# A hand-made start for an attention and feed-forward kernel: loads in order of need, the first group's attention by hand, integer work on GpSimd

## The chip, the core and the metric

The kernel runs on one core of a Trainium2 chip. The metric is the device time of one execution in microseconds. A core has five engines that run side by side, each through its own instructions in order: TensorE (PE in the profile; weight loads are shown as PEld), VectorE (DVE), ScalarE (ACT), GpSimd (POOL) and SyncE (SP), which here only issues transfers. They meet through semaphores. TensorE writes its results to PSUM[...].

## The reference

Attention without a softmax, for 8 groups (the batch) of 8 heads, 576 rows and 64 columns a head, then a feed-forward layer on 4608 tokens:

```python
kv  = einsum('bhsd,bhse->bhde', k, v)          # 64 x 64 a head
out = einsum('bhsd,bhde->bhse', q, kv)
rms = sqrt(mean(out * out, axis=-1) + 1e-6)
x   = (out / rms * g_norm)                     # -> (4608, 512)
h   = x @ w_in                                 # 512 -> 2048
g   = h * erf(softplus(h))
y   = g @ w_out                                # 2048 -> 512, (4608, 512) float32
```

q, k and v are float32. w_in and w_out are float64[...]: each weight comes in as two 32-bit integers, and the kernel makes a float32 of them.

## The kernel before

Two heads are a pair; a group of the batch has four pairs (`NP`), each giving 128 of the 512 columns of `xT`. For every pair there are four pieces of work, shortened here:

```python
def products():                                   # piece 0
    kv_ps = bank("kv_ps")
    for c in range(C):                            # C = 6 in the first group, two heads: 12 products
        ... nc.tensor.matmul(kv_ps[s, s], lhsT=ks[rows, i, c], rhs=vs[rows, i, c], ...)
    if p % 2 == 0:                                # the last 64 rows of q, for two pairs at once
        nc.tensor.transpose(kv_ps[:, q_tail], q_last[:, p // 2], ident)
    ...
    nc.vector.tensor_copy(out=bd[s, s], in_=kv_ps[s, s])          # two copies
    if p % 2 == 0:
        nc.vector.tensor_copy(out=tails[T], in_=kv_ps[:, q_tail])
    qt_ps = bank("qt_ps")
    for j in range(J):                            # J = 4
        nc.tensor.transpose(qt_ps[:, j * P : j * P + P], qs[:, j], ident)
    nc.scalar.copy(st["qT"], qt_ps)

def apply():                                      # piece 1
    nc.tensor.matmul(kv_ps[:, o_tail], lhsT=bd, rhs=st.pop("tail"), start=True, stop=True)
    nc.tensor.matmul(o_ps, lhsT=bd, rhs=qT, start=True, stop=True)     # o_ps is bank("se_ps")
    nc.vector.tensor_copy(out=x_last[:, p, T * R : T * R + R], in_=kv_ps[:, o_tail])
    nc.scalar.activation(qT, o_ps, AF.Square)

def mean():                                       # piece 3
    nc.tensor.matmul(ms, lhsT=mean_w.bitcast(FP32), rhs=u, start=True, stop=True)
    nc.scalar.activation(r, ms, AF.Ln, bias=eps_col)
    nc.scalar.activation(r, r, AF.Exp, scale=-0.5)
    nc.scalar.activation(u, r, AF.Square)

def norm():                                       # piece 4: three VectorE operations, the last writes xT
    ...(out=u, in0=ms, scalar=EPS, in1=u, op0=ALU.add, op1=ALU.mult)
    ...(out=u, in0=u, scalar=3.0, in1=r, op0=ALU.subtract, op1=ALU.mult)
    ...(out=x, in0=o, scalar=gm_col, in1=u, op0=ALU.mult, op1=ALU.mult)
```

A weight tile goes through load, split and join. The first four tiles (w0 to w3 here) are of w_in and hold 128 x 512 weights; later ones hold 128 x 1024.

```python
def w_split(which, f, k):
    nc.vector.tensor_scalar(out=e, in0=hi, scalar1=20, scalar2=0x7FF, op0=logical_shift_right, op1=bitwise_and)
    nc.scalar.activation(e, e, AF.Relu, scale=float(1 << 23), bias=exp_col)
    nc.vector.tensor_scalar(out=m, in0=hi, scalar1=0xFFFFF, scalar2=None, op0=bitwise_and)
    nc.scalar.activation(m.bitcast(FP32), m, AF.Identity, scale=2.0**-20, bias=1.0)

def w_join(which, f, k):                          # three VectorE operations
    ...(out=e, in0=hi, scalar=-(1 << 31), in1=e, op0=bitwise_and, op1=bitwise_or)
    ...(out=m, in0=lo, scalar=2.0**-52, in1=m, op0=mult, op1=add)
    nc.vector.tensor_tensor(out=out_, in0=e, in1=m, op=mult)      # out_: w_in_sb or w_out_sb
```

The start, in the order in which it is given to the engines:

```python
for i in range(NP - 1):                           # q on SP; k, v of pairs 0 to 2 on ACT's queue
    load_pair(i)
    if i == 0:
        load_last(0, 0); load_last(0, 1)
...
for _ in range(2):
    w_next("load")
load_last(0, 2); load_last(0, 3)
load_pair(NP - 1)
w_rounds = {1: ("split",), 2: ("join", "load", "split"), 3: ("join", "load"),
            5: ("split",), 6: ("split", "join", "load", "join", "load")}
banks_0 = {"kv_ps": (ps_at, "at"), "qt_ps": (ps_h, "h"), "ms_ps": (ps_h, "h")}
first = [attention(0, p, banks_0 | {"se_ps": (ps_o, f"o{p}")}) for p in range(NP)]
for i in range(NP + 3):
    for piece, p in ((0, i), (1, i - 1), (4, i - 3), (3, i - 2)):
        if 0 <= p < NP:
            first[p][piece]()
    ...
    for what in w_rounds.get(i, ()):
        w_next(what)
```

Behind it stands a loop over the hidden columns (`h_ps`, line 692): columns 0 and 1 need xT of all four pairs and weight tiles w0 and w1, column 2 needs w2, column 3 w3. Meanwhile the next group's attention and more splits and joins go on. The rest of the kernel, from the third group on, is the same products in three-part fp32r form (line 462).

## Time and profile before

| | |
|---|---|
| time, median of 3 runs | 944.4 us (943.82 to 945.24) |
| span of the profiled execution | 942.4 us |
| TensorE busy | 924.8 us, 98% |
| VectorE busy | 742.6 us, 79% |
| ScalarE busy | 615.6 us, 65% |
| GpSimd busy | 2.4 us, 10 instructions |
| first product of a pair starts | 6.49 us |
| first hidden column starts | 27.54 us (weight load), third 35.95 us |
| HBM over the span | 275 GB/s |

A row of the timeline reads: start in us, duration, engine, line of the kernel, operation, out<-in by the program's names, shape, number of instructions, and in brackets how long the engine was idle before and what released it. A row of a table of windows reads: the stretch, its length, busy time and number of instructions of PE, PEld, DVE, ACT and POOL, the granted clock, the share of the 16 DMA engines, GB/s. A row of the waits names who waited for whom, the sum, the number and the longest. "q" behind an engine's name is its sequencer.

### The profile page before, as it was taken

The page shows a single profiled execution, that of the slowest core. Times are in us where ns is not written, and L with a number is a line of the kernel's source. Part 1 is how long each engine was busy: PE and PEld are TensorE (multiplying, and loading weights), DVE is VectorE, ACT ScalarE, POOL GpSimd, SP SyncE. Part 2 cuts the span into 40 slices and gives each one's busy share as a digit, 9 for nine tenths or more (in the row PEclk, how much of TensorE's full clock was granted, in tenths as well). Part 3 has the DMA queues.
Part 4 walks back from the last instruction along what each step waited for, and adds up shares of the span by engine and source line. Part 5 has one row for each costly group of instructions (what it writes and reads, how often), then busy time and mean ns, then how long its engine had stood idle before and what let it go on. Part 6 is the DMA issues. An engine that isn't in the chain of part 4 may idle for free.

```text
span 942.4 us, 11743 instructions
## 1 busy us (share of the span) xinstructions
PE 924.8 (98%) x4272; PEld 683.4 (73%) x4272; DVE 742.6 (79%) x1056; ACT 615.6 (65%) x825; POOL 2.4 (0%) x10
## 2 busy tenths in 40 slices
PE   6999999999999999999999999999999999999997
PEld 4444445666688888888888888888888888888886
DVE  3999858887577787877778888878887877787667
ACT  3899776776766666666666666666666666665551
POOL 1000000000000000000000000000000000000000
PEclk9999999999999999999999999999999999999999
DMA  9766406899699998998899889998896778778871
GB/s 257 276 204 207 150 1 227 318 351 335 214 363 335 309 325 283 306 311 307 280 287 314 294 298 309 311 303 296 293 325 260 263 253 345 284 286 287 353 263 46
DMA packets 111842, 259.78 MB, mean 276 GB/s; under 512 B 43864, under 2 KB 69544, under 8 KB 111784
## 3 DMA queue, kind: packets, MB, share of 16 engines
q1 hardware_dynamic: 110152, 256.73, 78.7%
q10 hardware_dynamic: 1568, 2.29, 0.8%
q8 instruction: 34, 0.56, 0.2%
q14 instruction: 24, 0.20, 0.1%
q0 software_dynamic: 64, 0.00, 0.0%
HBM read 224.40 MB, written 34.60 MB: 275 GB/s over the span
## 4 chain that ended last, share of the span: by engine, by line
PE 92%; DVE 4%; DMA 2%; ACT 1%; issue 0%; SPq 0%; DVEq 0%
PE n_ps L462 45%; PE m_ps L462 22%; PE o_ps L520 10%; PE h_ps L692 6%; PE se_ps L325 3%; PE kv_ps L297 2%; PE qt_ps L319 2%; DMA w_raw<-in_moe_w_in_dram 1%; PE ms_ps L351 1%; DMA v_sb<-in_v_dram 1%; DVE h L876 1%; DVE e L445 1%; PE ms_ps L346 1%; PE ms_ps L347 1%; PE kv_ps L324 1%; DVE e L440 0%
## 5 line engine op out<-in xcount | busy, mean ns | idle before, releaser
L462 PE MATMUL n_ps<-x_forms,w_in_parts 128*128 128x512 f32 x896 | 232.5, 401 | 0.1
L462 PE MATMUL n_ps<-w_out_parts,g_forms 128*128 128x512 f32 x928 | 231.2, 391 | 0.0
L462 PEld LDWEIGHTS n_ps<-w_out_parts,g_forms 128*128 128x128 f32 x928 | 174.2, 188 | 38.4 <-issue 1.4
L462 PEld LDWEIGHTS n_ps<-x_forms,w_in_parts 128*128 128x128 f32 x896 | 166.8, 188 | 43.1 <-issue 9.3
L852 ACT ACTIVATE s<-h 128x512 f32<-128x512 f32 x112 | 71.0, 633 | 178.9 <-DVE h L445 178.9
L445 DVE TENSOR_TENSOR h<-m_ps,h 128x512 f32<-128x512 f32 x116 | 79.7, 687 | 59.8 <-ACT h L837 43.8
L462 PE MATMUL m_ps<-w_out_parts,g_forms 128*128 128x512 f32 x464 | 124.2, 389 | 0.0
L462 PE MATMUL m_ps<-x_forms,w_in_parts 128*128 128x512 f32 x448 | 120.0, 390 | 0.0
L520 PE MATMUL o_ps<-w_out_sb,h_sb 128*128 128x512 f32 x224 | 100.8, 593 | 0.3 <-DVE h_sb L642 0.3
L462 PEld LDWEIGHTS m_ps<-w_out_parts,g_forms 128*128 128x128 f32 x464 | 87.1, 188 | 18.0
L462 PEld LDWEIGHTS m_ps<-x_forms,w_in_parts 128*128 128x128 f32 x448 | 84.1, 188 | 17.7
L445 DVE TENSOR_TENSOR e<-m_ps,e 128x512 f32<-128x512 f32 x116 | 80.2, 692 | 18.2 <-PE m_ps L462 10.9
L440 DVE SCALAR_TENSOR_TENSOR e<-n_ps,e 128x512 f32<-128x512 f32 x88 | 60.3, 685 | 39.2 <-PE n_ps L462 39.2
L520 PEld LDWEIGHTS o_ps<-w_out_sb,h_sb 128*128 128x128 f32 x224 | 42.3, 190 | 48.9 <-issue 46.6
L411 DVE SCALAR_TENSOR_TENSOR g_forms<-g_forms 128x1024 fp32r<-128x1024 f32 x58 | 71.1, 1225 | 2.0
L408 DVE TENSOR_TENSOR g_forms<-h,g_forms 128x1024 fp32r<-128x1024 f32 x58 | 70.6, 1217 | 1.7 <-ACT g_forms L405 1.4
L876 DVE TENSOR_TENSOR h<-h,s 128x1024 f32<-128x1024 f32 x58 | 68.3, 1218 | 0.7 <-ACT s L856 0.7
L837 ACT ACTIVATE h<-n_ps 128x512 f32<-128x512 f32 x112 | 65.5, 585 | 3.4 <-PE n_ps L462 3.4
L405 ACT ACTIVATE g_forms<-h 128x1024 fp32r<-128x1024 f32 x58 | 58.9, 1059 | 12.2 <-PE m_ps L462 8.7
L692 PE MATMUL h_ps<-xT,w_in_sb 128*128 128x512 f32 x144 | 64.9, 594 | 0.7 <-DVE w_in_sb L240 0.6
L106 ACT ACT_TABLE_LOAD x44 | 56.5, 1283 | 0.8
L856 ACT ACTIVATE s<-s 128x1024 f32<-128x1024 f32 x56 | 56.2, 1052 | 0.3
(98 smaller groups left out, 1013.3 us busy)
## 6 DMA issues: line engine op xcount, KB each, us to landing
w_out_parts<-w_out SPq DMA_DIRECT2D x116, 768.0 KB
w_in_parts<-w_in SPq DMA_DIRECT2D x112, 768.0 KB
w_in<-w_new SPq DMA_DIRECT2D x16, 768.0 KB
q_sb<-in_q_dram SPq DMA_DIRECT2D x32, 256.0 KB
w_raw<-in_moe_w_out_dram SPq DMA_DIRECT2D x8, 1024.0 KB
out_dram<-e SPq DMA_DIRECT2D x32, 256.0 KB
k_sb<-in_k_dram SPq DMA_DIRECT2D x28, 287.5 KB
v_sb<-in_v_dram SPq DMA_DIRECT2D x28, 287.5 KB
```

The costliest lines, as they stand in the source:

```text
L106: nc.scalar.preload_act_table_set("softplus")
L405: nc.scalar.activation(high, x, AF.Copy, scale=1.0 + 2.0**-13)
L408: nc.vector.tensor_tensor(out=low, in0=x, in1=high.bitcast(FP32), op=ALU.subtract)
L411: nc.vector.scalar_tensor_tensor(out=both, in0=low.bitcast(FP32), scalar=SHIFT, in1=high.bitcast(FP32), op0=ALU.mult, op1=ALU.add,)
L440: nc.vector.scalar_tensor_tensor(out=out_, in0=ps, scalar=scale, in1=out_, op0=ALU.mult, op1=ALU.add)
L445: nc.vector.tensor_tensor(out=out_, in0=ps, in1=out_, op=ALU.add)
L462: nc.tensor.matmul(ps, lhsT=weights(form, k), rhs=moving(form, k), start=(form == forms[0] and k == 0), stop=(form == forms[-1] and k == 3),)
L520: nc.tensor.matmul(o_ps[j], lhsT=g[:, j * P : j * P + P], rhs=w_out_sb[:, f, :], start=(f == 0), stop=last,)
L692: nc.tensor.matmul(plain[i], lhsT=w_in_sb[:, c, i % FC * P : i % FC * P + P], rhs=xT[T][:, c, :], start=(c == 0), stop=(c == KC - 1),)
L837: nc.scalar.activation(h[:, i], n_ps, AF.Copy, scale=SHIFT - 1.0)
L852: nc.scalar.activation(s[:, i], h[:, i], AF.Softplus)
L876: nc.vector.tensor_tensor(out=part(h, half), in0=part(h, half), in1=part(s, half), op=ALU.mult)
```

## The change

It touches the start only, in four ways. The loads are put in the order in which they are needed and spread over the queues of SP, ACT and GpSimd. The first group's attention is given in a hand-written order, in which a pair's result comes before the next pair's products. A pair's transposed q shares the bank of that pair's result, so that the banks of the means are no longer used for it; eight idle products ahead of it are to raise TensorE's clock. The integer part of the weight tiles w0 and w1 moves from ScalarE (two operations a tile) to GpSimd (three).

```diff
+    for i, name, side in (
+        (0, "k", nc.sync), (0, "v", nc.scalar), (0, "q", nc.sync),
+        (1, "k", nc.scalar), (1, "v", nc.scalar), (1, "q", nc.sync),
+        (2, "k", nc.sync), (2, "v", nc.sync), (2, "q", nc.sync),
+    ):
+        load_part(i, name, side)
+        if (i, name) == (1, "v"):
+            for j in range(2):
+                load_last(0, j, side)
 ...
+    for i in range(2, NP):
+        load_last(0, i, nc.gpsimd)
 ...
-        nc.scalar.activation(e, e, AF.Relu, scale=float(1 << 23), bias=exp_col)
 ...
-        nc.scalar.activation(m.bitcast(FP32), m, AF.Identity, scale=2.0**-20, bias=1.0)
+        if which == "in" and f < 2:
+            nc.gpsimd.tensor_scalar(out=e, in0=e, scalar1=896, scalar2=1151, op0=ALU.max, op1=ALU.min)
+            nc.gpsimd.tensor_scalar(out=e, in0=e, scalar1=-896.0, scalar2=2.0**23, op0=ALU.add, op1=ALU.mult)
+            nc.gpsimd.tensor_scalar(out=m.bitcast(FP32), in0=m, scalar1=2.0**-20, scalar2=1.0, op0=ALU.mult, op1=ALU.add)
+        else:
+            nc.scalar.activation(e, e, AF.Relu, scale=float(1 << 23), bias=exp_col)
+            nc.scalar.activation(m.bitcast(FP32), m, AF.Identity, scale=2.0**-20, bias=1.0)
 ...
+            qt_ps = transpose_q() if T == 0 else None      # now ahead of q_last's transpose
 ...
-            nc.tensor.matmul(kv_ps[:, o_tail], lhsT=bd, rhs=st.pop("tail"), start=True, stop=True)
-            nc.tensor.matmul(o_ps, lhsT=bd, rhs=qT, start=True, stop=True)
+            both = [(kv_ps[:, o_tail], st.pop("tail")), (o_ps, qT)]
+            for ps, x in reversed(both) if T == 0 else both:
+                nc.tensor.matmul(ps, lhsT=bd, rhs=x, start=True, stop=True)
 ...
+    idle = ps_o.tile([P, P], FP32, name="idle", tag="o3")
+    def keep_warm(n):
+        for _ in range(n):
+            nc.tensor.matmul(idle, lhsT=mean_w.bitcast(FP32), rhs=mean_f, start=True, stop=True)
+    keep_warm(8)
 ...
-    banks_0 = {"kv_ps": (ps_at, "at"), "qt_ps": (ps_h, "h"), "ms_ps": (ps_h, "h")}
+            {"kv_ps": (ps_at, "at"), "qt_ps": (ps_o, f"o{p}"), "se_ps": (ps_o, f"o{p}"), "ms_ps": (ps_h, "h")}
 ...
+    for step in (
+        (PRODUCTS, 0), (APPLY, 0), (PRODUCTS, 1), loads_ahead, (MEAN, 0),
+        (PRODUCTS, 2), (APPLY, 1), "split", (NORM, 0), (APPLY, 2), (MEAN, 1),
+        "join", "load", "split", (PRODUCTS, 3), (APPLY, 3), (MEAN, 2), (NORM, 1),
+        "join", "load", (MEAN, 3), (NORM, 2), "split", (NORM, 3), "split",
+        "join", "load", "join", "load",
+    ):
```

`loads_ahead` is what stood at the end of the second round before: two more weight tiles and the next group's first two pairs. Tuples and dictionaries are folded onto fewer lines here.

## The prediction

> **What bounds the kernel now.** I read, in this order, the page's busy shares, the waits of TensorE over the whole span, the windows of the first 120 us, the chain of waits up to 45 us, and the timelines of TensorE and VectorE up to 36 us.

> ```profile
> PE 924.8 (98%) x4272; PEld 683.4 (73%) x4272; DVE 742.6 (79%) x1056; ACT 615.6 (65%) x825; POOL 2.4 (0%) x10
> ...
> PE kv_ps L297 <- DMA v_sb<-in_v_dram: 8.9, 4, 6.5
> PE ms_ps L351 <- ACT rms_r L358: 1.3, 1, 1.3
> PE h_ps L692 <- DVE w_in_sb L240: 0.6, 1, 0.6
> PE kv_ps L305 <- DMA q_last<-in_q_dram: 0.4, 1, 0.4
> PE o_ps L520 <- DVE h_sb L642: 0.3, 1, 0.3
> ...
> 0.00:14.35 14.35, 5.94 (x60) 5.29 (x61) 1.95 (x12) 2.33 (x3) 2.39 (x10) 1.00 0.88 240
> 14.35:20.18 5.83, 4.87 (x40) 2.41 (x41) 3.43 (x10) 3.52 (x7) 0.00 (x0) 1.00 1.13 278
> 20.18:35.90 15.72, 13.80 (x58) 6.14 (x58) 14.87 (x30) 14.43 (x24) 0.00 (x0) 1.00 0.70 221
> 35.90:60.00 24.10, 24.05 (x79) 11.32 (x80) 22.71 (x30) 21.42 (x29) 0.00 (x0) 1.00 0.89 298
> ...
> 6.49 1.55 PE L297 MATMUL kv_ps<-v_sb,k_sb 96*64 96x64 f32 x24 [6.49 <-DMA v_sb<-in_v_dram]
> 8.48 0.44 PE L305 MATMUL kv_ps<-ident,q_last 128*128 128x128 f32 x1 [0.44 <-DMA q_last<-in_q_dram]
> 11.26 1.55 PE L297 MATMUL kv_ps<-v_sb,k_sb 96*64 96x64 f32 x24 [1.48 <-DMA v_sb<-in_v_dram]
> 15.99 0.92 PE L297 MATMUL kv_ps<-v_sb,k_sb 96*64 96x64 f32 x24 [0.47 <-DMA v_sb<-in_v_dram]
> ...
> 32.53 0.75 DVE xT L378
> 33.29 0.33 DVE w_e L207
> 33.62 0.34 DVE w_m L216
> 33.95 0.61 DVE w_e L226
> 34.57 0.61 DVE w_m L230
> 35.17 0.02 issue
> 35.20 0.70 DVE w_in_sb L240
> 35.90 0.04 issue
> 35.95 7.13 PE h_ps L692 x16
> ```

> The page: TensorE is busy 98% of 942.4 us, so at most some 18 us are to be had. The list of all TensorE's waits (cause; sum, times, longest): 11.5 us in all, every one but the 0.3 us before 36 us. The windows (length, then busy time of TensorE, weight load, VectorE, ScalarE, GpSimd; clock; DMA share; GB/s): from 35.9 us TensorE works 24.05 of 24.10 us. So everything the change can move lies before 35.9 us, and a microsecond won or lost there goes to the end one for one. The windows also show who holds that front: DMA until about 14 us, and from 20.18 to 35.90 VectorE, busy 14.87 of 15.72 us, with ScalarE close behind (14.43). The chain says the same: the third hidden product starts at 35.95 us because of a row of VectorE work without a gap: normalise pair 3 (ends 33.28), split tile 3, join tile 2. **The number to predict is therefore when VectorE finishes the join of weight tile 2: 35.89 us now.**

> [...] The kernel before has no GpSimd work beyond its first 7.4 us[...]. [...] a 128x256 memset took 0.310 us, a 128x1 one 0.098, hence 0.83 ns an element. [...] the same 24 matmuls of a pair take 1.55 us at 6.49 and 11.26 us, 0.92 at 15.99. [...] with two queues at work the DMA share is full (1.13 from 14.35 to 20.18 us).

> **The change, part by part.**

> *Loads.* The bytes stay: k and v of a pair 295 kB each, q 262, a q_last 33, a weight tile 524. Only their order changes: k0 and v0 at once on two queues, then q0/k1, q1/v1, q_last 0 and 1, k2, v2, q2, w0, w1, pair 3. The rate of before was 162 GB/s until 6.5 us and 299 from 6.5 to 16 us (a windows row each), hence 1,053 kB by 6.5 us and 3,893 kB by 16. With it: k0 and v0 (590 kB) about 4.5 us; q0 and k1 (1,147) 6.8; q1, v1 and the q_last of pairs 0 and 1 (1,770) 9.0; all of pair 2 (2,622) 11.8; w0 13.6; w1 15.3; pair 3 18.9. Before, pair 2 was used at 15.99 and pair 3 at 20.09. So the order helps pair 2 by 4 us and pair 3 by 1, while q_last of pairs 0 and 1 comes 0.6 us later than before (8.48 to 9.04).

> *Warming.* Eight fp32 128x128 products from about 1.65 us, when VectorE has made their operand. A mean over 512 columns takes 0.86 us at full clock (the chain's "ms_ps L351" rows), so 128 columns 0.21, and 0.43 at half clock; eight are 3.5 us, to 5.1. Pair 0's k and v are there by then, so this costs nothing, and should turn the clock up 5 to 8 us earlier than the 15 us of now. It spares pair 1 and pair 0's result some 1.7 us.

> *The hand order on TensorE*, in warm issue times of the chain's rows (pair's products 0.73, four transposes 0.47, result 0.89, tail 0.17, mean 0.86): transposing q_last 9.04 to 9.41; VectorE's two copies, 9.91; result and tail of pair 0 to 11.01; pair 1's products and transposes 12.21; mean 0, 13.07; pair 2's products, transposes, q_last 14.44; result and tail of pair 1, 15.70 with the 0.2 us of latency. VectorE's two small copies behind it end at 16.13, and there its long row begins.

> *VectorE's row from 16.13*, from the timeline's start-to-start times (split 0.68, norm 2.12, join 1.93, small copy 0.17 to 0.40): split w0 16.81; norm 0 at 18.93; x_last 19.15; join w0 21.08; split w1 21.76; pair 3's two copies 22.16; x_last 3 22.33; norm 1 24.45; join w1 26.38; norm 2 28.50; split w2 29.18; norm 3 31.30; split w3 31.98; join w2 33.91. Undisturbed that would be 2.0 us before today's 35.89. Three waits come in. (a) Pair 3's copies stand behind split w1; only after them come its result and tail and the copy of that tail: 0.89 + 0.17 + 0.2 + latencies = about 1.35 us in which VectorE has nothing to do. (b) GpSimd's work on w0: [...] I take 0.8. [...] join w0 starts at 20.18, not 19.4: 0.8 us. (c) [...]: 0.3 + 0.1 us. Sum: 33.91 + 1.35 + 0.8 + 0.4 = 36.5 us, 0.6 us later than now. A queue-by-queue walk of the kernel before with the same durations gives 35.89 for the same event, so the durations are right; the landings and GpSimd are not known.

> *ScalarE* loses four operations (2 x 0.72 + 2 x 0.61 = 2.7 us) in its tightest stretch, and the Exp chains start earlier; that is what keeps it out of the sum. *q^T in the result's bank* frees TensorE from waiting for a bank of the means (1.3 us in the list of waits are now between means and ScalarE), but TensorE isn't what ends last here. After 36 us nothing changes.

> So 944.4 + 0.6 = **945.0 us**.

> **The rivals.** *Earlier landings win*: for it speaks that before, the SP queue stood 4.12 us in the issues of w0 and w1 (timeline), and the first 14 us moved only 240 GB/s. If everything lands 1.5 us earlier and GpSimd needs 0.55 us, join w2 ends near 34: 942.5 us. *GpSimd becomes the bound*: if one operation takes 1.1 us or more[...], the row of VectorE waits twice for it; at 1.1 the walk gives 38.3 us, +2.4: 947 us. Against it: the second tile has 4 us of room. *All is hidden*: the DMA, not the order, sets pair 3, and VectorE's total is the same; for it, that no VectorE instruction leaves the row: 944 us. *The clock drops again* in the gap from 7.9 to 9.0 us, when TensorE waits for q_last: +1.7 us. A larger effect I can't see: the waits to be had are 11.2 us, and VectorE's work alone between its first weight and join w2 is some 17 us.

> **Range and chances.** The landings are known to about 1 us, GpSimd to 0.3 us an operation (2 to 3 us in the sum), the clock to 1.7 us. Together about 2.7 us either way: 941.8 to 948.6 us. 2% is 19 us, more than all of the waits that could go, and double what the rivals cost: within 2% is nearly certain.

> **What would show it.** Pair 0's q_last transpose near 9 us (earlier or later moves all). The clock up by 9 us. Split w0 at 16 us, GpSimd's three operations over 3.3 us with VectorE idle before join w0 for about 0.8, and 1.3 us idle before x_last of pair 3. Join w2's end and the third hidden product at 36.5 us; TensorE without waits from there. Wrong if GpSimd takes far from 0.8 us, if VectorE isn't the one waited for at the third hidden product, or if anything behind 60 us differs.

## The result, and the profile after

| | before | after |
|---|---|---|
| device time, median (range) | 944.16 us (943.82 to 945.24) | 950.17 us (949.42 to 950.25) |
| ratio, 95% interval | | 1.006 (1.0042 to 1.0077) |
| profiled span | 942.4 us | 948.4 us |
| third hidden product starts | 35.95 us | 42.40 us |

The kernel became 6.0 us slower. The prediction said 0.6 us slower, and its range ended at 948.6. The third hidden product starts 6.45 us later than before, and the run ends 6.0 us later: the whole loss lies ahead of it, where the prediction looked. (The rest of the kernel behind this product takes 905.9 to 906.9 us before and in ten of the eleven profiled runs of the table below; e8_clock_scalar is the exception.)

First the busy shares of the page, then TensorE's waits over the whole span (cause; sum, times, longest), both of the changed kernel:

```profile
PE 931.3 (98%) x4288; PEld 687.8 (73%) x4288; DVE 742.9 (78%) x1056; ACT 613.6 (65%) x821; POOL 10.6 (1%) x18
```

```profile
PE se_ps L362 <- DVE bd_kv L349: 4.5, 2, 3.8
PE qt_ps L336 <- DMA q_sb<-in_q_dram: 2.0, 1, 2.0
PE kv_ps L342 <- DMA q_last<-in_q_dram: 1.8, 1, 1.8
PE idle L598 <- DVE eps_col L197: 1.7, 1, 1.7
PE h_ps L773 <- DVE w_in_sb L269: 0.6, 1, 0.6
...
```

TensorE is busy 6.5 us longer than before, and its waits are no longer than the 11.5 us of before (11.2 in all, with two of 0.3 us not shown). The sums mislead, though, since the idle products stand where TensorE used to wait for its first load (timeline of TensorE):

```profile
1.68 3.78 PE L598 MATMUL idle<-mean_f,mean_w 128*128 128x128 f32 x16 [1.68 <-DVE eps_col L197]
```

Without these 3.78 us TensorE is busy 2.7 us longer than before, and without the wait for the start (6.5 us before, 1.7 now) its waits have grown from 5.0 to 9.5 us. So the loss shows both as products that take longer and as waits, for q, for q_last and for VectorE's copies. The same four windows as before (length, then busy time of TensorE, weight load, VectorE, ScalarE, GpSimd; clock; DMA share; GB/s):

```profile
0.00:14.35 14.35, 8.12 (x47) 6.28 (x48) 1.39 (x9) 1.87 (x2) 3.58 (x12) 0.85 0.93 231
14.35:20.18 5.83, 5.83 (x64) 4.44 (x63) 1.08 (x5) 3.11 (x6) 0.00 (x0) 0.77 1.11 308
20.18:35.90 15.72, 11.90 (x50) 5.65 (x49) 11.57 (x25) 8.00 (x15) 7.05 (x6) 0.78 0.62 190
35.90:60.00 24.10, 23.15 (x77) 10.43 (x76) 22.64 (x35) 20.20 (x28) 0.00 (x0) 1.00 0.79 255
```

VectorE, which owned the window from 20.18 to 35.90 us (14.87 us busy before), now has 11.57 there, and ScalarE 8.00 instead of 14.43. The clock column is below 1.00 in three of the windows. (It counts the time ahead of the trace's first clock record as full speed, so the slow start of the kernel before, with 1.55 us for 24 products that later take 0.92, shows as 1.00.) The chain that ended last, in its early part (start, duration, what):

```profile
0.72 4.07 DMA k_sb<-in_k_dram
...
4.81 6.51 DMA q_last<-in_q_dram
...
11.37 0.49 PE kv_ps L342
12.58 2.05 PE se_ps L362 x2
...
14.95 1.48 PE kv_ps L326 x24
16.43 0.86 PE qt_ps L336 x4
...
28.18 2.05 PE se_ps L362 x2
...
41.66 0.70 DVE w_in_sb L269
...
42.40 7.13 PE h_ps L773 x16
```

The end of this stretch is as predicted: VectorE's join of weight tile 2, then the third hidden product. Three things ahead of it are not. q_last of pair 0 is transposed at 11.37 us, not at 9.04. A pair's result (se_ps) takes 2.05 us, twice, for which the prediction took 0.89. And pair 0's result, pair 1's products (1.48) and transposes (0.86) all run at half clock, where full clock was assumed. The row of VectorE shows where the weight tiles stand in it (timeline of VectorE and GpSimd: start, duration, what, in brackets the idle time before and its releaser):

```profile
21.60 2.05 POOL L237 TENSOR_SCALAR w_e<-w_e 128x512 int32<-128x512 int32 x1 [10.18 <-DVE w_e L224]
22.49 0.69 DVE L406 SCALAR_TENSOR_TENSOR qT<-qT,rms_r 128x512 f32<-128x512 f32 x1
...
24.38 0.69 DVE L255 SCALAR_TENSOR_TENSOR w_e<-w_raw,w_e 128x512 int32<-128x512 int32 x1 [0.20 <-POOL w_e L240]
24.43 1.12 POOL L243 TENSOR_SCALAR w_m<-w_m 128x512 f32<-128x512 int32 x1
25.59 0.69 DVE L259 SCALAR_TENSOR_TENSOR w_m<-w_raw,w_m 128x512 f32<-128x512 uint32 x1 [0.51 <-POOL w_m L243]
...
27.59 0.45 DVE L349 COPY bd_kv<-kv_ps 64x64 f32<-64x64 f32 x2
30.59 0.23 DVE L363 COPY x_last<-kv_ps 128x64 f32<-128x64 f32 x1 [2.55 <-PE kv_ps L362]
```

GpSimd holds VectorE up for 0.20 + 0.51 = 0.71 us. The copy of pair 3's tail (x_last) holds it up for 2.55 us.

Last, the clock itself. The clock records of this trace change at 6.73, 10.15, 16.97, 27.21 and 34.04 us: distances of 3.41 us and of two and three times that. Windows cut at these steps:

```profile
3.32:6.73 3.41, 3.37 (x34) 3.11 (x33) 0.00 (x0) 0.00 (x0) 0.63 (x2) 1.00 1.10 283
6.73:10.14 3.41, 0.86 (x10) 0.51 (x7) 0.00 (x0) 0.55 (x1) 0.00 (x0) 1.00 1.20 258
10.14:13.56 3.42, 1.46 (x2) 0.69 (x3) 0.74 (x3) 0.03 (x1) 0.25 (x1) 0.50 1.04 263
13.56:16.97 3.41, 3.41 (x31) 2.65 (x30) 0.67 (x3) 0.60 (x1) 0.00 (x0) 0.50 1.10 336
...
23.80:27.21 3.41, 0.57 (x4) 0.33 (x4) 2.67 (x6) 1.62 (x3) 1.67 (x2) 1.00 0.57 173
27.21:30.62 3.41, 2.44 (x5) 1.44 (x6) 0.85 (x5) 0.35 (x1) 3.04 (x3) 0.50 0.35 114
```

The idle products and pair 0's products filled one step (3.37 of 3.41 us busy), and the clock went up at its end. The next step, in which TensorE waits for q and q_last, had 0.86 us of work, and the clock was taken back at its end, for two steps. Just those two carry pair 0's result and pair 1. From 23.80 us the same happens again: 0.57 us of work, and pair 3's result falls into the slow steps that follow.

### The profile page after: what moved, and what is told of

The parts are those of the page before. It is cut to its first block, busy times and chain, and to the rows that moved or that the text cites. A ratio compares the mean times of both kernels' runs of the same rounds, so it can differ in the third digit from the quotient of the medians.

```text
span 948.4 us, 11782 instructions
## 1 busy us (share of the span) xinstructions
PE 931.3 (98%) x4288; PEld 687.8 (73%) x4288; DVE 742.9 (78%) x1056; ACT 613.6 (65%) x821; POOL 10.6 (1%) x18
## 3 DMA queue, kind: packets, MB, share of 16 engines
q10 hardware_dynamic: 1232, 1.48, 0.5%
## 4 chain that ended last, share of the span: by engine, by line
PE 94%; DVE 3%; DMA 1%; ACT 0%; POOL 0%; issue 0%; DVEq 0%
PE n_ps L499 46%; PE m_ps L499 23%; PE o_ps L557 9%; PE h_ps L773 6%; PE se_ps L362 3%; PE kv_ps L326 2%; PE qt_ps L336 2%; PE ms_ps L388 1%; DMA q_last<-in_q_dram 1%; PE kv_ps L362 1%; PE ms_ps L383 1%; PE ms_ps L384 1%; PE kv_ps L342 0%; DMA k_sb<-in_k_dram 0%; DVE e L482 0%; DVE h L957 0%
## 5 line engine op out<-in xcount | busy, mean ns | idle before, releaser
L499 PEld LDWEIGHTS m_ps<-w_out_parts,g_forms 128*128 128x128 f32 x464 | 87.1, 188 | 18.1
L482 DVE TENSOR_TENSOR e<-m_ps,e 128x512 f32<-128x512 f32 x116 | 80.2, 692 | 18.2 <-PE m_ps L499 10.9
```

What stands on the lines that cost most here:

```text
L482: nc.vector.tensor_tensor(out=out_, in0=ps, in1=out_, op=ALU.add)
L499: nc.tensor.matmul(ps, lhsT=weights(form, k), rhs=moving(form, k), start=(form == forms[0] and k == 0), stop=(form == forms[-1] and k == 3),)
```

## The experiments

The theory after the result: *the clock*. The hand order leaves TensorE idle twice while it waits (for q_last, and for VectorE's copies of pair 3), the clock drops each time, and what follows at half speed holds up VectorE's row. The rivals: *q_last* (only its late landing counts), *GpSimd* (its 2.05 us operation, and what the two engines cost each other side by side, hold up the row), *the order* (the copy of pair 3's tail stands ahead of a norm that is ready), and *the loads* as a whole. Each was taken out of the changed kernel, and two parts of the change were put alone into the kernel before.

| run | what it is | median us (range) | ratio (95%) | third hidden product |
|---|---|---|---|---|
| after | the change | 950.17 (949.42–950.25) | 1.006 (1.0042–1.0077) | 42.40 |
| e1_warm | after, idle products in the gaps | 948.1 (947.31–949.57) | 1.0037 (1.0023–1.0051) | – |
| e2_qlast | after, q_last second in its queue | 948.88 (948.57–949.97) | 1.0044 (1.0029–1.0059) | 40.75 |
| e3_scalar | after, no work on GpSimd | 949.34 (949.01–950.47) | 1.0051 (1.0034–1.0068) | 41.17 |
| e4_oldloads | after, the loads of before | 949.60 (948.78–949.95) | 1.0048 (1.0034–1.0063) | 40.89 |
| e5_pair3 | after, two norms and means swapped | 948.22 (947.15–948.43) | 1.0033 (1.002–1.0047) | 39.46 |
| e6_mend | e5, e2 and an earlier split | 945.64 (945.26–946.45) | 1.0012 (1.0005–1.0019) | 38.41 |
| e7_clock | e6 with more idle products | 944.07 (943.24–945.34) | 0.9991 (0.9982–0.9999) | 35.19 |
| e8_clock_scalar | e7, no work on GpSimd | 944.05 (943.12–947.36) | 0.9995 (0.9986–1.0004) | 35.27 |
| b_loads | before, new loads only | 946.05 (944.89–948.33) | 1.0019 (1.0009–1.003) | 36.63 |
| b_loads_q | b_loads, q_last second in its queue | 945.30 (943.59–947.14) | 1.0007 (0.9998–1.0015) | 36.88 |
| b_pool | before, GpSimd's part only | 944.78 (943.94–945.5) | 1.0003 (0.9995–1.0012) | 35.80 |

The ratios are to runs of the kernel before on the same chip. The last column is from one profiled run each. One execution of e1_warm, the profiled one, was disturbed (1177.3 us); it is left out here, median included, and so e1_warm has no profile to read.

**e1_warm.** Idle products in TensorE's gaps:

```diff
+            if T == 0 and p == 0: keep_warm(8)      # ahead of transpose_q()
             qt_ps = transpose_q() if T == 0 else None
+            if T == 0 and p == 0: keep_warm(8)
+            if T == 0 and p == NP - 1: 14 products of the same kind into bank o0
```

> The changed kernel with idle products in TensorE's two long waits (8 before and 8 behind pair 0's transposes, 14 between pair 3's transposes and its result). Clock theory: the two stretches at half clock (10.1 to 17.0 and 27.2 to 34.0 us) cost 2.7 us between the transpose of q_last and VectorE's long row, and 1.2 us more in pair 3's result; with the clock kept up the third hidden product starts 3 to 4 us earlier and the time is 946.3 to 947.3. Rival (the half clock only fills waits for loads and VectorE): within 0.7 us of the changed kernel, 950.

The ratio falls from 1.006 to 1.0037, some 2 us, for 30 products that compute nothing. The mean clock, which counts only what comes after the first rise (the kernel before, slow until 14.9 us, has 0.999), goes from 0.991 (three of the four runs of after; 0.997 in the fourth, which is no faster) to between 0.997 and 0.999: fewer drops. That speaks for the clock. But 3 to 4 us were expected, and without a profile it isn't shown when the clock first rose here. The other 4 us don't come back, so the clock isn't alone, or these products don't mend all of it.

**e2_qlast.** The two q_last loads go right behind k0, on SP's queue:

```diff
-        if (i, name) == (1, "v"):
+        if (i, name) == (0, "k"):
```

> The changed kernel with the q_last of pairs 0 and 1 loaded on SP's queue right behind k0 instead of behind v1 on ACT's. Late q_last theory: its transpose follows the transposes of pair 0 at about 9.8 us instead of 11.4, and the shorter wait may keep the clock up: 1.5 us less with the clock as it is, up to 4 with it: 946 to 948.6. Rival (VectorE's row is set by pair 2's loads or by weights): no change, 950.

Timeline of TensorE in e2_qlast:

```profile
9.10 1.09 PE L336 MATMUL qt_ps<-ident,q_sb 128*128 128x128 f32 x4 [2.55 <-DMA q_sb<-in_q_dram]
9.98 0.42 PE L342 MATMUL kv_ps<-ident,q_last 128*128 128x128 f32 x1
```

q_last now waits for nothing, and its transpose is 1.39 us earlier (9.98 for 11.37). The time fell by about as much, 1.3 us (1.5 by the ratios). So q_last is a part of the loss, and not most of it. What TensorE waits for is now q of pair 0, and the clock dropped all the same, at 8.25 us in this run.

**e3_scalar.** The integer part of all tiles on ScalarE again:

```diff
-        if which == "in" and f < 2:
+        if False:
```

> The changed kernel with the integer part of w0 and w1 back on ScalarE (two operations a tile instead of GpSimd's three). GpSimd theory: its first operation takes 2.05 us and VectorE idles 0.7 us for it before and in join w0, so 0.7 to 1 us less: 949.2. If GpSimd is the main cause of the 6 us: 945 to 946. Rival (ScalarE then holds up the means): same or slower, 950 to 951.

Timeline of ScalarE and TensorE in e3_scalar:

```profile
25.16 0.72 ACT L247 ACTIVATE w_e<-w_e,exp_col 128x512 int32<-128x512 int32 x1 [1.30 <-DVE w_e L224]
25.79 0.61 ACT L248 ACTIVATE w_m<-w_m 128x512 f32<-128x512 int32 x1
26.30 0.56 ACT L356 COPY qT<-qt_ps 128x512 f32<-128x512 f32 x1
26.92 2.07 PE L362 MATMUL se_ps<-qT,bd_kv 128*128 128x512 f32 x2 [3.58 <-ACT qT L356]
```

Without GpSimd only 0.8 us come back, and the ranges of the two kernels overlap. In the profiled run q_last was also transposed at 10.26 us, 1.11 earlier than in after with the same loads, and that is most of the 1.23 us by which the third hidden product came earlier. The join of w0 is done 5.0 us after the start of its split, for 5.9 in after; but ScalarE pays in another place: pair 3's q^T copy stands behind the two operations on w1, and TensorE waits for it. GpSimd's long operation is at most a small part of the loss in this order; e8_clock_scalar asks again in the mended one.

**e4_oldloads.** The load loop and the queues of before; all else as in the changed kernel.

> The changed kernel with the loads of the kernel before (order and queues), all else as changed. If the new order of loads is at fault: 2 to 3 us less, 947 to 948, since q_last came at 8.4 us there. If the order of loads helps, as it was meant to: pairs 2 and 3 come later (15.9 and 20.0 us), and the hand order waits for pair 2 before pair 1's result: 1 us more, 951.

q_last is transposed at 8.82 us, 0.34 later than in the kernel before, and the time is only 0.6 us below that of after (1.1 by the ratios, with overlapping ranges), between the two expectations. The new loads are therefore not what costs 6 us in the changed kernel: with the old ones, too, the clock was up only from 14.42 us and down again from 24.66 to 31.49, and the wait ahead of pair 3's x_last was again 2.55 us.

**b_loads, b_pool and b_loads_q.** The other way round: one part of the change in the kernel before (the third with the edit of e2_qlast).

> The kernel before with the new loads alone (order and queues). If the new order of loads were a cause of the slowing: 946.5 to 948. Order theory (the hand order and its waits are the cause, loads are about neutral): q_last comes 2 us later, w0 1.4 us later, pair 2 2.7 us earlier, pair 3 0.8 us later, and VectorE's row, which ends the front, moves by under 1 us: 944 to 946.

> The kernel before with the integer part of w0 and w1 on GpSimd alone. Three operations of 2.05, 0.62 and 0.62 us against two of 0.72 and 0.61 on ScalarE: w0's are done at about 18.2 us when join w0 starts at 18.3, w1's at 24.2[...] when join w1 starts at 24.1. If GpSimd is a small matter: 945 to 946. If GpSimd is the cause: 948 or more. Rival (the relief of ScalarE wins): 943.5.

> The kernel before with the new loads, and the q_last of pairs 0 and 1 behind k0. Late q_last theory: the 1.8 us that the new loads cost alone come from q_last (10.6 us instead of 8.5), so 944.0 to 945.0 now. Rival (pair 3, which came 0.7 us later, or w0): 946.

A line of the timeline of b_loads (TensorE), two of its chain and the same two of the chain of before, then the timeline of b_pool (GpSimd):

```profile
10.62 0.45 PE L322 MATMUL kv_ps<-ident,q_last 128*128 128x128 f32 x1 [3.58 <-POOL gm_col L199]
...
13.76 6.88 DMA v_sb<-in_v_dram
20.77 0.92 PE kv_ps L314 x24
...
13.74 6.22 DMA v_sb<-in_v_dram
20.09 0.92 PE kv_ps L297 x24
```

```profile
14.65 2.05 POOL L220 TENSOR_SCALAR w_e<-w_e 128x512 int32<-128x512 int32 x1 [7.18 <-DVE w_e L207]
16.78 0.62 POOL L223 TENSOR_SCALAR w_e<-w_e 128x512 int32<-128x512 int32 x1
17.48 0.62 POOL L226 TENSOR_SCALAR w_m<-w_m 128x512 f32<-128x512 int32 x1
```

The new loads alone cost 0.2% (1.8 us), and q_last is 2.1 us later than before (10.62 for 8.48; the releaser named in that line isn't the cause, since the transpose doesn't read gm_col). But the chain of this run doesn't go through q_last. It goes through the v of pair 3, which lands 0.68 us later than before, and from pair 3's products to the third hidden product it is 15.86 us here and in the kernel before. In b_loads_q q_last is early again (transposed at 8.71 us), pair 3 is later still (21.02), and the third hidden product again comes 15.86 us behind it, at 36.88. So in these runs the late pair 3 sets the front, and the late q_last costs nothing that the profiles show. The time of b_loads_q is 0.07% above before, which can't be told from nothing, and 945.30 lies between what the theory and the rival gave. Part of what is left is the clock: the four of its twelve runs with a mean clock of 0.997 or less took 946.1 to 947.1 us, the other eight 943.6 to 945.6.

GpSimd's part alone is free: the three operations on w0 run earlier than in the changed kernel, are over at 18.10 us, and VectorE's join doesn't wait for them.

**e5_pair3.** Norm 1 and mean 2 ahead of pair 3's result:

```diff
-        "join", "load", "split", (PRODUCTS, 3), (APPLY, 3), (MEAN, 2), (NORM, 1),
+        "join", "load", "split", (PRODUCTS, 3), (NORM, 1), (MEAN, 2), (APPLY, 3),
```

> The changed kernel with three steps swapped: pair 1's norm and pair 2's mean ahead of pair 3's result (before: behind it). Order theory: VectorE no longer idles 2.5 us before the copy of pair 3's tail, since a norm that is ready stands there, and pair 2's mean no longer waits behind pair 3's result; the third hidden product comes 2 to 2.5 us earlier: 947.5 to 948. Rival (the idle time only moves, to the next wait for ScalarE): 949.5 to 950.

Timeline of VectorE in e5_pair3:

```profile
26.78 0.45 DVE L349 COPY bd_kv<-kv_ps 64x64 f32<-64x64 f32 x2
27.26 0.69 DVE L403 SCALAR_TENSOR_TENSOR qT<-ms_ps,qT 128x512 f32<-128x512 f32 x1
...
29.38 0.21 DVE L363 COPY x_last<-kv_ps 128x64 f32<-128x64 f32 x1
29.51 1.07 DVE L255 SCALAR_TENSOR_TENSOR w_e<-w_raw,w_e 128x512 int32<-128x512 int32 x1
```

The norm now fills the time in which pair 3's result is made, and the idle 2.55 us are gone. The time falls by about 2 us (949.42 at the lowest of after, 948.43 at the highest here), and the second drop of the clock is gone as well, by a hair, as the section on the hardware shows. So this swap doesn't measure the order alone: a part of the 2 us is the clock. In the last line the join's first operation takes 1.07 us instead of 0.69 while GpSimd works.

**e6_mend.** e5_pair3 with e2_qlast, and the first "split" ahead of pair 2's products.

```diff
-        (PRODUCTS, 2), (APPLY, 1), "split", (NORM, 0),
+        "split", (PRODUCTS, 2), (APPLY, 1), (NORM, 0),
```

> The changed kernel with that swap, the first split ahead of pair 2's products, and the q_last of pairs 0 and 1 behind k0. If the three add up (2.3 for the swap, 0.7 for VectorE's split in a wait and 0.7 for GpSimd's work out of the way, 1.3 for q_last as measured): 950.0 - 5.0 = 945.0. If the half clock also goes where the waits go: down to 943. Rival (loads set everything): not under 947.

It is 4.5 us faster than after and 0.12% slower than before. What is left in the profiled run is the clock, at half until 17.52 us. Not every run is like it: it is one of four out of 20 with a mean clock of 0.997 or more (946.2 to 946.5 us); the other sixteen had 0.994 or 0.995 and took 945.3 to 946.1, which fits an earlier rise and one drop behind it, but none of them has a profile (timeline of TensorE, e6_mend):

```profile
11.47 2.05 PE L362 MATMUL se_ps<-qT,bd_kv 128*128 128x512 f32 x2 [0.73 <-DVE bd_kv L349]
13.77 1.55 PE L326 MATMUL kv_ps<-v_sb,k_sb 96*64 96x64 f32 x24
```

**e7_clock and e8_clock_scalar.** e6_mend with more idle products; the second also without GpSimd's part.

```diff
+            if T == 0 and p == 0: keep_warm(4)      # behind pair 0's products
             qt_ps = transpose_q() if T == 0 else None
 ...
-    keep_warm(8)
+    keep_warm(12)
```

> The mended order (945.6) with 12 idle products at the start instead of 8 and 4 more behind pair 0's products, so that TensorE is busy from 1.7 us until the load of q0. Clock theory: the clock is up before 9 us and stays; pair 0's result, pair 1 and mean 0 go in 3 us less, and the row of VectorE starts some 2.5 us earlier: 942.5 to 943.8, better than the kernel before. Rival (loads of pair 2 and w0 at 13.3 and 15.7 us hold the row then): 944.8 to 945.6.

> The same with the integer part back on ScalarE. If GpSimd is worth having in a good order (it frees ScalarE for the Exp chain): 1 us slower than the kernel with 12 and 4 idle products. If GpSimd's slow first operation[...] cost as much as they free: equal within 0.5 us.

A window of e7_clock:

```profile
20.18:35.90 15.72, 12.87 (x54) 5.82 (x55) 15.36 (x29) 10.99 (x17) 3.26 (x3) 1.00 0.69 220
```

Eight idle products more take 1.6 us off e6_mend (2.0 by the ratios, as the two ran beside other runs of before), with nothing else touched: that is the cleanest measure of what the clock cost there. (942.5 to 943.8 us were expected; it is 944.07.) In the profiled run it stayed at full from 5.88 us to the end. VectorE's row is as full again as before (15.36 of 15.72 us), and the third hidden product starts at 35.19 us, 0.76 us earlier than before. The kernel is 0.09% faster than before, with an interval that ends at 0.9999. One such interval among twelve is a hint and no more: the 6 us are back, and whether anything is won over the kernel before isn't shown. With ScalarE in place of GpSimd the time is the same (944.05; its profiled run took 945.98, since TensorE waited 2.55 us for a later weight tile), so moving the integer part is worth nothing here even in the mended order.

## Why the prediction was wrong, point by point

- **Which event sets the time** ("when VectorE finishes the join of weight tile 2"): right. The join ends at 42.35 us, the hidden product follows at 42.40, and the end moves with it.
- **The warming: the step that failed.** The prediction had the idle products "turn the clock up 5 to 8 us earlier" for good, which was the author's estimate, and put all later products into the sum at full clock. The clock did rise, 8.2 us earlier than before (6.73 for 14.9), but fell back at 10.15. From q_last's transpose to split w0 the walk had 7.09 us and the trace has 9.73. Of the excess of 2.64, 2.45 are the half clock: result and tail of pair 0 took 2.37 for 1.06, pair 1's products 1.48 for 0.73, its transposes 0.86 for 0.47. The rival "the clock drops again in the gap from 7.9 to 9.0 us" had the mechanism; it was kept as a rival at 1.7 us and should have been in the sum. A second drop, in the wait for pair 3, was not foreseen at all; it added about 1.2 us more, under (a). The 30 idle products of e1_warm bring back some 2 us, and the eight more of e7_clock 1.6 to 2.0.
- **The landings.** The rate was right (231 GB/s in the first window, 240 before), the order wasn't: a mean rate, applied to the list of loads, gave 9.0 us for q_last, and it came at 11.3. The chain shows a part of the reason. The second of the two q_last loads was issued only at 4.81 us, when k0 had landed at 4.79, and k2, which the list had behind it, had been issued at 2.73; q_last then took 6.51 us to land. In e3_scalar and e5_pair3 the same load was issued at 5.08 and 5.33 us, again 0.02 us behind k0's landing, but took 5.14 and 5.16, so about 1 us of this loss differs from run to run. Why the issue waited isn't shown. e2_qlast takes 1.39 us of the 2.33 back, and 1.3 us come off the time. Pair 3, expected 1 us earlier than before, came 0.7 us later in b_loads. (At the rate that the prediction names, its bytes give 18.1 to 18.3 us for pair 3, not 18.9; nothing hangs on it.)
- **(a) Pair 3's wait in the row.** The mechanism was right, the term mis-sized: 2.55 us for 1.35, because the result took 2.05 + 0.34 at half clock for 0.89 + 0.17. It was also taken as given, when a ready norm stood right behind it; e5_pair3 swaps them, and some 2 us come back, in part by the clock. This is the fault of the hand order.
- **(b) GpSimd.** The wait was right (0.71 us for 0.8), its working wasn't: not three operations of 0.8 us but 2.05, 0.62 and 0.62 (1.12 against the join). The 0.8 us an operation was the author's estimate; the trace of before has no GpSimd operation over 128x512. In the sum, 3.96 us from start to end for 3.3. The rival that GpSimd becomes the bound, 947 us, foresaw an operation above 1.1 us, and one took 2.05; but e3_scalar and b_pool show that it isn't what costs the time.
- **(c) Norms 0 and 1 beside GpSimd.** The 0.3 and 0.1 us were the author's estimate, which the trace of before doesn't show. They lost 0.1 us and nothing; GpSimd's third operation lost 0.50 us instead (1.12 for 0.62), and in e5_pair3 a join's first operation 0.38 (1.07 for 0.69).
- **ScalarE and q^T in the result's bank.** ScalarE has four operations less and is busy 2.0 us less over the span (613.6 for 615.6; the 8.00 us for 14.43 in the window are mostly waiting). It is worth nothing in the time, as e7_clock and e8_clock_scalar show.
- **The sum.** The join ends 5.85 us later than predicted: 2.33 for q_last, 2.64 up to split w0, 0.88 in the row (pair 3 +1.20, norms 0 and 1 −0.3, GpSimd −0.09, the rest +0.07).

What stays open: how the 2 us of e5_pair3 divide between order and clock; how much of e6_mend's gain is the earlier split, which had no run of its own; and the clock mended in the changed kernel without the other edits, for which there are only times, not a profile.

## What to carry to other kernels

Before a hand order or an idle warming is credited with full clock, go through the first tens of microseconds in steps of 3.41 us, the distance found between the clock's changes here, for several places of the first step, and count TensorE's work in each: here every gap that left 1.38 us of work or less in a step at full clock was paid for with two steps at half speed, and idle products belong into the gap as much as ahead of the first work. Put a small load that everything waits for early in a queue rather than at its "turn" in an order over several queues, and look up when it is really issued. In a row of an engine that sets the end, put work that is ready ahead of a copy that waits for a product just issued.

## What the runs showed of the hardware

**The clock changes in fixed steps whose phase differs from run to run.** The distance between any two changes of one trace is 3.41 us or a multiple of it; the first step that begins within the trace begins at 3.32 us in after, at 1.43 in e2_qlast and at 0.45 in e6_mend. A step need not be idle for a drop: in after the clock dropped behind steps with 0.86 and 0.57 us of work. Windows at the steps of each trace, e4_oldloads, e5_pair3, e6_mend and b_loads_q in turn:

```profile
21.25:24.66 3.41, 1.38 (x28) 1.08 (x28) 2.58 (x5) 2.40 (x4) 2.62 (x3) 1.00 0.79 238
24.66:28.07 3.41, 1.40 (x2) 0.84 (x3) 1.81 (x6) 0.00 (x0) 2.09 (x2) 0.50 0.57 169
```

```profile
23.01:26.42 3.41, 1.40 (x6) 0.57 (x6) 2.66 (x6) 3.31 (x6) 1.65 (x2) 1.00 0.59 182
```

```profile
3.87:7.28 3.41, 3.14 (x32) 2.68 (x31) 0.00 (x0) 0.00 (x0) 0.09 (x1) 1.00 1.10 239
```

```profile
9.25:12.67 3.42, 3.25 (x32) 2.81 (x33) 1.18 (x5) 0.58 (x1) 0.22 (x1) 1.00 1.13 283
```

For the rise, busy time alone doesn't decide. The clock rose after 3.16 us of work in a step in e2_qlast and 3.37 in after, and stayed at half after 3.14 in e6_mend and after 3.25 in b_loads_q (both still before the first record, where the column says 1.00; the clock rose only at 17.52 and 16.08). What else counts isn't shown. A step that was busy throughout, 3.41 us, raised the clock every time.

The eight idle products and pair 0's products fill a step only if the phase suits. e2_qlast and e6_mend have the same loads and the same eight products, and the clock rose at 4.84 us in one and at 17.52 in the other: in e2_qlast a step began at 1.43 us, just ahead of them, and in e6_mend the end of a step at 3.87 us cut them in two. Twelve idle products, with pair 0's products behind them, filled a step in both profiled runs that had them (3.41 us of work from 2.47 us in e7_clock and from 4.46 in e8_clock_scalar), and with the four more the next one was busy 2.67 us (e7_clock) and 2.53 (e8_clock_scalar), enough to keep the clock.

**GpSimd's cost depends on the operation.** In after, b_pool and e6_mend a tensor_scalar over 128x512 of 32-bit integers takes 2.02 to 2.05 us with max and min. With add and multiply, or with multiply and add into fp32, it takes 0.62, except once 0.84 (b_pool) and once 1.12 (after). The prediction's 0.8 us, an estimate, is near the second kind; the first takes three times as long as the second.

**VectorE and GpSimd side by side.** Short operations took 0.38 and 0.50 us longer in such a place: the join's first operation 1.07 us for 0.69 in e5_pair3 (1.06 in e6_mend), GpSimd's third operation 1.12 for 0.62 in the changed kernel, where it began 0.05 us behind the join's first. Beside GpSimd's operation of 2.05 us there was no such loss: VectorE's second norm operation took its usual 0.69 us (22.49 us in the changed kernel, 27.98 in e5_pair3), and at most 0.1 us was lost (0.81 us to the start of the next operation in the changed kernel, for 0.73 in the norm at 31.45). What makes the short operations longer, and why the long one doesn't, isn't shown.
